# A recurrent attention and a routed expert layer on one core: experts in an order found on the chip, with a size for each place

## The chip, the cores and the metric

The program runs on one core of a Trainium2 chip, as one launch. The time is that of the launch in device microseconds; three runs of the kernel before took 530.75, 531.43 and 537.21 us, a median of 531.43 us. The core has TensorE (PE, matmuls; its weight loads have a row of their own, PEld), VectorE (DVE), ScalarE (ACT), GpSimd (POOL) and SyncE (SP, which only issues transfers here).

## What is computed

```python
# r, k, v: (4, 8, 768, 48); w, u: (8, 48); 8 experts, w1 (8, 384, 1024), w2 (8, 1024, 384), all float32
for t in range(S):                                    # attention, one state per batch and head
    y[:, :, t] = einsum('bhd,bhde->bhe', rt, state + (u * kt) outer vt)
    state = w * state + kt outer vt
x = y.transpose(0, 2, 1, 3).reshape(3072, 384)
logits = (x / |x|) @ (emb / |emb|).T / tau            # (3072, 8)
idx = argmax(logits);  gate = softmax(logits)[idx]
for e in range(8):
    h = maximum(x[idx == e] @ w1[e], 0)
    out[idx == e] = gate * (h @ w2[e])
```

Each of the 3072 tokens goes to exactly one expert.

## The kernel before

**Attention.** The sequence is cut into 6 groups of 128 positions (NCH, the index c), and each group into two turns of two batches (12 turns, index t). A turn scales and transposes R and K (scale_r, scale_k, turn_in, take_in, own_r), forms scores, masks them (mask, own_terms), adds the outer products of K and V to the state (outer, half_state, next_state), multiplies with V and with the state (with_v in two phases, with_state), and turns the result back into rows (take_y, turn_y, take_x), which keep_x stores to the array xs in HBM. The order of all this is written out by hand: attention() gives every function a planned time in a table (plan.at), and the functions are issued in the order of these numbers; on each engine the instructions then run strictly in that order, each waiting for what it reads.

**Routing.** After each second turn the 512 tokens of a group are routed: logits and take_logits (lgT), turn_logits and keep_logits (lg), choose (largest logit; VectorE steps mx, l, er, back, oh, a running count in counts), ranks (two small matmuls that count the tokens of the same expert before each token), placed (rank), places (tile and slot), gate, places_b (the one-hot arrays QV and P), put (matmuls that scatter token numbers and gates into lists) and collect (adds them to lists). The routing of a group is spread over the next turns; that of the last group has nothing beside it, and ends in take, the table of token numbers for each expert and tile.

**Experts.** Every expert has room for 512 tokens, four tiles of 128 (TM = 4); a place that no token fills has a number beyond the array and is skipped by the transfers. For each expert GpSimd gathers four tiles of rows from xs (gather, tiles G), TensorE transposes them (turn_x, three banks of four transposes, each copied by VectorE to xTe), layer1 does 8 x 3 matmuls with 512 columns into hT (ReLU on ScalarE), layer2 does 4 x 8 matmuls with 384 columns into the banks pu, VectorE scales by the gate, and GpSimd scatters the rows to the output. The order on TensorE is layer1(e), turn_x(e+1), layer2(e). The weights have two buffers. Those of experts 0 and 1 load in 14 pieces during turns 4 to 8 of the attention, those of expert e+2 as soon as layer1(e) and layer2(e) have let go of the buffer.

**The end.** needs() counts the tokens of each expert with one matmul and compares them with 512 x g; again() turns that into a flag that every engine loads into a register (line 963), and a branch that is not taken where all tokens had room (line 964). The branch holds a slow path for the tokens that did not fit.

## Time and profile before

| | us |
|---|---|
| median of three runs | 531.43 |
| the profiled execution | 535.02 |
| its span in the profile | 533.2 |
| TensorE busy in the span | 483.6 (91%) |
| VectorE, ScalarE, GpSimd busy | 143.9, 106.2, 137.5 |
| chain that ended last, layer 1 (L733) and layer 2 (L744) | 31% and 31% of the span |

The profile is one execution. A row names a line of the kernel, an engine, an operation and the tiles it writes and reads; times are microseconds from the start of the span. The releaser of a wait is inferred, and a wait that nothing in the profile explains is called "issue". The chain of work that ended last is followed back from the end, at each step to what released it.

### The profile page before, as it was taken

The numbers are of one execution on the slowest core, as the hardware profiler recorded it, in microseconds if no ns is written. First come the engines' busy times: TensorE is split into PE (matmuls) and PEld (weight loads), VectorE is DVE, ScalarE is ACT, GpSimd is POOL, SyncE is SP. The second block draws the span as 40 slices with busy tenths as digits, with TensorE's granted clock in tenths as the row PEclk, the third lists the DMA queues.
The fourth block names the chain that finished last, engine by engine and source line by source line (L and its number), as shares of the span: only waits on it lengthen the run. The fifth ranks groups of instructions, "written<-read, shape, count | busy, mean of one in ns | idle before, by whom it ended". The sixth has DMA issues, their size and how long they took to land.

```text
span 533.2 us, 10611 instructions
## 1 busy us (share of the span) xinstructions
PE 483.6 (91%) x4523; PEld 299.4 (56%) x4523; DVE 143.9 (27%) x390; ACT 106.2 (20%) x247; POOL 137.5 (26%) x167
## 2 busy tenths in 40 slices
PE   7889879888963999999999999999999999999990
PEld 3778768777852445545545545544554554554550
DVE  5656666676842110002001101101000200110010
ACT  1335535363450120020020021011012002002100
POOL 4447545355304401400310130230140110020010
PEclk9679999898995899999999999999999999999995
DMA  9938797994111312403223043142150330000000
GB/s 178 194 70 190 151 263 169 259 218 129 43 62 44 85 52 97 162 14 135 100 97 133 29 161 119 45 165 75 73 180 1 134 121 26 15 30 0 9 35 8
DMA packets 95515, 54.29 MB, mean 102 GB/s; under 512 B 78781, under 2 KB 90110, under 8 KB 95458
## 3 DMA queue, kind: packets, MB, share of 16 engines
q1 hardware_dynamic: 88658, 43.67, 29.6%
q0 software_dynamic: 4096, 9.45, 4.9%
q8 instruction: 37, 0.61, 0.5%
q10 hardware_dynamic: 2704, 0.40, 0.4%
q14 instruction: 20, 0.16, 0.1%
HBM read 45.63 MB, written 11.01 MB: 106 GB/s over the span
## 4 chain that ended last, share of the span: by engine, by line
PE 79%; DVE 8%; issue 3%; POOL 1%; DMA 1%; ACT 1%; POOLq 0%; DVEq 0%; ACTq 0%
PE ps L733 31%; PE pu L744 31%; PE ps L302 3%; PE pu L363 2%; PE py L724 2%; PE py L414 2%; PE ps L328 2%; PE py L433 2%; PE pu L448 1%; PE pu L596 1%; PE py L474 1%; DVE P L588 1%; DVE xTe L725 1%; DVE AT L342 1%; DVE RT L315 1%
## 5 line engine op out<-in xcount | busy, mean ns | idle before, releaser
L733 PE MATMUL ps<-xTe,w 128*128 128x512 f32 x384 | 167.6, 596 | 0.0
L744 PE MATMUL pu<-w,hT 128*128 128x384 f32 x512 | 166.4, 486 | 0.0
L744 PEld LDWEIGHTS pu<-w,hT 128*128 128x128 f32 x512 | 96.7, 190 | 66.2 <-issue 0.5
L733 PEld LDWEIGHTS ps<-xTe,w 128*128 128x128 f32 x384 | 73.6, 192 | 90.8 <-issue 89.0
L750 POOL DMA_INDIRECT out_dram<-y,take x32 | 31.8, 993 | 281.3 <-DVE y L749 277.2
L736 ACT ACTIVATE hT<-ps 128x512 f32<-128x512 f32 x64 | 38.2, 597 | 300.5 <-PE ps L733 300.5
L749 DVE TENSOR_SCALAR y<-pu,lists 128x384 f32<-128x384 f32 x32 | 19.7, 617 | 165.5 <-PE pu L744 165.5
L725 DVE COPY xTe<-py 128x512 f32<-128x512 f32 x24 | 15.9, 688 | 153.0 <-PE py L724 152.7
L711 POOL DMA_INDIRECT G<-xs,take x32 | 32.6, 1020 | 15.9 <-issue 8.2
L286 POOL TENSOR_TENSOR Rw<-R,rpow 128x384 f32<-128x384 f32 x24 | 24.8, 1034 | 22.1 <-PE ps L328 8.7
L328 PE MATMUL ps<-RT,KT 48*64 48x128 f32 x768 | 27.8, 297 | 0.8 <-issue 0.7
L328 PEld LDWEIGHTS ps<-RT,KT 48*64 48x64 f32 x768 | 24.3, 148 | 3.3 <-issue 2.7
L282 POOL TENSOR_TENSOR Kw<-K,kpow 128x384 f32<-128x384 f32 x24 | 25.5, 1062 | 0.0
L724 PE MATMUL py<-ident,G 128*128 128x128 f32 x96 | 15.6, 298 | 8.0 <-DMA G<-xs,take 5.5
L302 PE MATMUL ps<-ident,Rw 128*128 128x128 f32 x96 | 17.4, 306 | 3.7 <-POOL Rw L286 2.1
L309 ACT COPY RT<-ps 128x512 f32<-128x512 f32 x24 | 14.1, 586 | 30.9 <-PE ps L302 30.9
L315 DVE TENSOR_TENSOR RT<-ps,uw 128x512 f32<-128x512 f32 x24 | 16.4, 687 | 13.5 <-ACT RT L309 13.4
L724 PEld LDWEIGHTS py<-ident,G 128*128 128x128 f32 x96 | 11.7, 149 | 14.6 <-DMA G<-xs,take 6.5
L414 PE MATMUL py<-AT,V 64*64 64x64 f32 x768 | 18.8, 238 | 1.0 <-ACT peek L402 0.6
L342 DVE TENSOR_TENSOR AT<-ps,smask 128x256 f32<-128x256 f32 x48 | 17.8, 410 | 4.9 <-PE ps L328 4.9
L363 PE MATMUL pu<-V,Kw 64*64 64x48 f32 x704 | 15.6, 235 | 3.9 <-DVE full L550 2.0
L390 POOL TENSOR_TENSOR T<-T,wC 128x384 f32<-128x384 f32 x10 | 8.3, 827 | 40.2 <-DVE T L384 37.5
(142 smaller groups left out, 337.9 us busy)
## 6 DMA issues: line engine op xcount, KB each, us to landing
w<-in_moe_w_dram SPq DMA_DIRECT2D x24, 512.0 KB, 5.1
w<-in_moe_w_dram SPq DMA_DIRECT2D x32, 384.0 KB, 4.2
K<-in_k_dram SPq DMA_DIRECT2D x24, 192.0 KB, 4.0
V<-in_v_dram SPq DMA_DIRECT2D x24, 192.0 KB, 3.8
xs<-X SPq DMA_DIRECT2D x24, 192.0 KB, 2.9
R<-in_r_dram SPq DMA_DIRECT2D x22, 192.0 KB, 3.9
G<-xs,take POOLq DMA_INDIRECT x32, 3.4
out_dram<-y,take POOLq DMA_INDIRECT x32, 2.6
```

Of the source, the lines that this page charges most:

```text
L282: k.nc.gpsimd.tensor_mul(of(k.Kw, t)[:, u, :, 0:D], of(k.K, t)[:, u], k.kpow)
L286: ins = k.nc.gpsimd.tensor_mul(of(k.Rw, t)[:, u, :, 0:D], of(k.R, t)[:, u], k.rpow)
L302: k.nc.tensor.transpose(bank[:, p * C : (p + 1) * C], pair(src[:, u], p), k.ident)
L328: ins = k.nc.tensor.matmul(k.D[2 * u + par][halves(s), p * C : (p + 1) * C], KT[rows, u, p, halves(s)], RT[rows, u, p, s].rearrange("q j i ...
L363: k.nc.tensor.matmul(k.U[s][par * DP : (par + 1) * DP, col : col + D], Kw[halves(s), u, h, :], V[halves(s), u, h, 0:D], start=True, stop=T ...
L414: k.nc.tensor.matmul(y_out(k, par, p, u, s), V[halves(s), u, 2 * p + par, :], AT[halves(s), u, par, p * HC : (p + 1) * HC], start=first an ...
L711: k.nc.gpsimd.indirect_dma_start(out=G[:, :], out_offset=None, in_=k.xs[:, :], in_offset=IndirectOffsetOnAxis(ap=k.take[:, e, t : t + 1], ...
L724: k.nc.tensor.transpose(ps[:, t * 128 : (t + 1) * 128], G[:, m * 128 : (m + 1) * 128], k.ident)
L733: k.nc.tensor.matmul(ps, w1[:, m, f * 128 : (f + 1) * 128], xT[:, m, :], start=(m == 0), stop=(m == NK - 1))
L736: k.nc.scalar.activation(hT[:, f, :], ps, ACT.Relu)
L744: k.nc.tensor.matmul(ps, hT[:, f, t * 128 : (t + 1) * 128], w2[:, f, :], start=(f == 0), stop=(f == NF - 1))
L750: k.nc.gpsimd.indirect_dma_start(out=k.out[:, :], out_offset=IndirectOffsetOnAxis(ap=k.take[:, e, t : t + 1], axis=0), in_=y[:, :], in_off ...
```

## The change

The eight experts are run in an order that the chip finds, and each place j of the order has a fixed size, CAPS[j], in place of 512. After group 3 of the six the two experts with the fewest tokens so far become places 0 and 1 (settle, early); after group 4 the others follow by falling count, so that the largest sizes, 432, 416 and 400, stand at places 2 to 4. The order is a one-hot array; from it VectorE works out the experts' numbers (which), SyncE loads them into registers, and the weights are fetched at an address that the register gives (weights). The embeddings, the tie order, the running counts and the lists are put into the order by products and sums on VectorE (sort_embeddings, sort_counts, sort_lists), so that the last group routes straight into places. Expert 0's weights are now issued at the end of turn 10, expert 1's after the transposes of expert 0's rows. Sizes that are not whole tiles do layer 2 with the weights stationary and the rows streaming; their result yT is transposed back after the next expert's layer 1 (turn_out). needs compares the counts with the sizes.

The plan of the last turns and of the routing of groups 4 and 5 is written anew: outer and half_state of turn 11 stand at 4.1 and 4.5 of their turn where they stood at 4.75 and 5.6, and the 14 functions that routed group 5 one after another become a table of 17.

```diff
@@
+CAPS = (384, 384, 432, 416, 400, 384, 384, 384)
+EARLY = 2
+TILES = [-(-n // 128) for n in CAPS]
...
@@ def choose(k, c):
+def choose(k, c, rev=None):
...
+def scale(k, c):
+    inv = k.rt.tile([128, B], F32, name="inv", tag="inv")
+    k.nc.vector.reciprocal(inv, k.ssq[c % 2])
+    k.nc.vector.tensor_mul(k.shifted, k.shifted, over_e(inv))
...
@@ def ranks(k, c):
+    if c in SETTLE:
+        mm(bank[:, B * E : (B + 1) * E], k.ones, k.counts[:, :, B], start=True, stop=True)
...
+SETTLE = (NCH - 3, NCH - 2)
+def count(k, c):
+    k.nc.vector.scalar_tensor_tensor(
+        k.key, bank_of(k, "ranks", c)[:, B * E : (B + 1) * E], float(E), k.index if c == SETTLE[0] else k.rev,
+        ALU.mult, ALU.add,
+    )
+def settle(k, c):
...
+    if not early:
+        nc.vector.tensor_scalar(low, k.few, float(EARLY), -float(2 * E * N), ALU.is_lt, ALU.mult)
+        nc.vector.tensor_add(k.key, k.key, low)
+    nc.vector.tensor_tensor(
+        wins, k.key[:, None, :].to_broadcast(square), k.key[:, :, None].to_broadcast(square),
+        ALU.is_lt if early else ALU.is_gt,
+    )
+    nc.vector.reduce_sum(at, wins, axis=AX.X)
...
+def settled(k):
...
+    for j in range(js.start, js.stop):
+        k.expert[j] = k.nc.values_load(
+            k.which[0:1, j : j + 1], engines=(mybir.EngineType.SP,), min_val=0, max_val=E - 1,
...
+def in_order(k, out, a, n):
+    k.nc.vector.tensor_mul(
+        t, a[:, :, None, :].to_broadcast(shape), k.order[:, None, :, :].to_broadcast(shape)
+    )
+    k.nc.vector.reduce_sum(out, t, axis=AX.X)
+def sort_embeddings(k):
+    in_order(k, k.ent_sorted[:, :, 0:E], k.ent[:, :, 0:E], 4)
+def sort_counts(k):
+    in_order(k, k.rev_sorted[:, None, :], k.rev[:, None, :], 1)
+    in_order(k, k.cum[:, None, :], k.counts[:, None, :, B], 1)
+def sort_lists(k):
+    old, k.lists = k.lists, k.lists_sorted
+    shape = [128, E, 2 * TM, E]
...
@@ def attention(k):
-    for e in range(2):
-        for i, piece in enumerate(pieces(k, e, k.weights[e])):
-            plan.at((4 + 2 * e) * P + 1.0 + i * 4.0, piece)
+    plan.at((TURNS - 2) * P + 8.1, weights, k, 0)
...
+            plan.at(at + 4.1, outer, k, t)
+            plan.at(at + 4.5, half_state, k, t)
...
+def weights(k, j):
+    w1, w2 = k.weights[j]
+    e = bass.ds(k.expert[j], 1)
...
+def rows_in(e, t):
+    return min(128, CAPS[e] - 128 * t)
...
@@ def layer1(k, e):
-                ps, w1[:, m, f * 128 : (f + 1) * 128], xT[:, m, :], start=(m == 0), stop=(m == NK - 1)
+                ps, w1[:, m, f * 128 : (f + 1) * 128], xT[:, m, 0:n], start=(m == 0), stop=(m == NK - 1)
...
@@ def layer2(k, e):
+    for m in range(NK):
+        ps = k.U[m % 2][:, 0:n]
         for f in range(NF):
             k.nc.tensor.matmul(
+                ps, w2[:, f, m * 128 : (m + 1) * 128], hT[:, f, 0:n], start=(f == 0), stop=(f == NF - 1)
             )
+        k.nc.vector.tensor_copy(k.yT[:, m, 0:n], ps)
+def turn_out(k, e):
+    if CAPS[e] % 128 == 0:
+        return
+    for t in range(TILES[e]):
+        ps, n = k.U[t % 2][:, 0:DM], rows_in(e, t)
+        for m in range(NK):
+            k.nc.tensor.transpose(
+                ps[0:n, m * 128 : (m + 1) * 128], k.yT[:, m, t * 128 : t * 128 + n], k.ident
+            )
+        finish(k, e, t, ps)
...
@@ def experts(k):
+    ins = turn_x(k, 0)
+    after(k, weights(k, 1), ins)
     for e in range(E):
+        layer1(k, e)
+        if e:
+            turn_out(k, e - 1)
         if e + 1 < E:
             turn_x(k, e + 1)
...
@@ def needs(k, first):
+    nc.vector.tensor_tensor(many, cp[0:1, :], k.caps[0:1, :], ALU.is_gt)
+    nc.vector.tensor_mul(need, need, many[:, :, None].to_broadcast([1, E, TG]))
+    nc.vector.tensor_mul(
+        by, need.rearrange("o j g -> o g j")[:, None].to_broadcast(shape),
...
+    nc.vector.reduce_sum(need, by, axis=AX.X)
```

Three places, as the instructions stand in each engine's queue. The first is VectorE in the routing of the last group, from the running counts to the first step of places. Before:

```order
L521 SCALAR_TENSOR_TENSOR counts<-on,cum_oh 128x40
L523 RECIPROCAL inv<-ssq_139 128x4
L524 TENSOR_TENSOR l<-l,inv 128x32
L550 TENSOR_TENSOR full<-pu_62,cum_oh 128x32
L551 TENSOR_REDUCE rank<-full 128x4
L560 TENSOR_TENSOR over<-rank,level 128x16
```

and now (lists_sorted is the list in the new order):

```order
L546 SCALAR_TENSOR_TENSOR counts<-on,cum_oh 128x40
L655 TENSOR_TENSOR lists_by<-lists,order 128x512
L659 TENSOR_REDUCE lists_sorted<-lists_by 128x64
L665 TENSOR_TENSOR full<-ps_59,cum_oh 128x32
L666 TENSOR_REDUCE rank<-full 128x4
L675 TENSOR_TENSOR over<-rank,level 128x16
```

The reordering of the lists has moved in front of full, which reads the ranks, and the scaling inv and l has moved behind. The second is VectorE in the routing of group 4, from rank on. Before:

```order
L524 TENSOR_TENSOR l<-l,inv 128x32
L550 TENSOR_TENSOR full<-pu_62,cum_oh 128x32
L551 TENSOR_REDUCE rank<-full 128x4
L560 TENSOR_TENSOR over<-rank,level 128x16
L564 TENSOR_REDUCE hi<-over 128x4
L566 SCALAR_TENSOR_TENSOR lo<-hi,rank 128x4
L567 TENSOR_TENSOR over<-slot,hi 128x16
```

and now:

```order
L666 TENSOR_REDUCE rank<-full 128x4
L598 TENSOR_SCALAR low<-at 128x8
L599 TENSOR_TENSOR key<-key,low 128x8
L601 TENSOR_TENSOR wins<-key 128x64
L606 TENSOR_REDUCE at<-wins 128x8
L609 TENSOR_TENSOR order<-at,slot 128x48
L636 TENSOR_TENSOR by_turn<-ent,order 128x256
L639 TENSOR_REDUCE ent_sorted<-by_turn 128x4x8
L636 TENSOR_TENSOR by_turn<-rev,order 128x64
L639 TENSOR_REDUCE rev_sorted<-by_turn 128x8
L636 TENSOR_TENSOR by_turn<-counts,order 128x64
L639 TENSOR_REDUCE cum_oh<-by_turn 128x8
```

Between rank and the rest (over and what follows it) stand eleven operations that find the order and apply it, and after these rows come two more for the numbers in which. The third is TensorE at the end of the attention, where the logits of group 5 (L474, now L491) are formed and turned. L596 and L714 are puts, L448 and L465 the turn of YT_126 back into rows. Before:

```order
L596 MATMUL pu_63<-QV,P 128x64 x4
L448 MATMUL pu_62<-ident,YT_126 128x128 x4
L448 MATMUL pu_63<-ident,YT_126 128x128 x4
L474 MATMUL py_64<-YT_125,ent 32x128 x2
L474 MATMUL py_64<-YT_126,ent 32x128 x2
```

and now:

```order
L491 MATMUL py_64<-YT_126,ent_sorted 32x128 x2
L714 MATMUL ps_60<-QV,P 128x64 x4
L465 MATMUL pu_62<-ident,YT_126 128x128 x4
L465 MATMUL pu_63<-ident,YT_126 128x128 x4
L510 MATMUL ps_58<-ident,lgT 128x128
L574 MATMUL ps_59<-cum_oh,umask 128x32
```

The put of group 4 and the last turn of YT_126 have moved from ahead of the logits to behind them, ahead of the transpose of lgT.

## Rows read from the trace of the kernel before

**Rows 1.** Table by stage: start:end, length, engines' busy us (instructions), granted clock, DMA.

```profile
core 0: us, PE busy (x) PEld busy (x) DVE busy (x) ACT busy (x) POOL busy (x), PEclk, DMA share, GB/s
...
148.00:166.00 18.00, 10.66 (x227) 9.02 (x223) 9.68 (x46) 6.84 (x22) 1.27 (x2) 0.85 0.13 46
...
219.20:262.50 43.30, 42.95 (x126) 22.69 (x125) 4.45 (x7) 4.78 (x8) 8.06 (x8) 1.00 0.28 101
...
100.00:120.00 20.00, 18.18 (x548) 16.04 (x544) 12.31 (x39) 10.93 (x30) 7.33 (x9) 0.94 0.94 236
```

**Rows 2.** Chain that ended last, 174 to 243 us: start, duration, engine, tile, line.

```profile
174.76 22.09 PE ps L733 x48
...
198.73 20.64 PE pu L744 x64
219.37 20.60 PE ps L733 x48
239.97 0.45 PE py L724 x4
...
240.45 0.70 DVE xTe L725
...
241.19 0.66 PE py L724 x4
```

**Rows 3.** Timeline of VectorE, 141 to 150 us: start, duration, operation, [idle before, releaser].

```profile
141.85 0.29 DVE L482 COPY lgT<-py 128x128 f32<-128x128 f32 x1 [0.48 <-PE py L474]
...
143.25 0.68 DVE L588 TENSOR_TENSOR P<-slot,lo 128x512 f32<-128x512 f32 x1
...
148.76 0.56 DVE L379 TENSOR_TENSOR Tmid<-T,pu 128x384 f32<-128x384 f32 x1 [1.95 <-PE pu L363]
```

**Rows 4.** Timeline of VectorE, routing of the last group.

```profile
157.61 0.29 DVE L482 COPY lgT<-py 128x128 f32<-128x128 f32 x1 [1.86 <-PE py L474]
158.38 0.19 DVE L491 COPY lg<-pu 128x32 f32<-128x32 f32 x1 [0.48 <-PE pu L486]
...
159.75 0.24 DVE L521 TENSOR_TENSOR_SCAN counts<-on,cum_oh 128x40 f32<-128x40 f32 x1
...
162.39 0.43 DVE L582 TENSOR_TENSOR QV<-HV,cum_oh 128x256 f32<-128x256 f32 x1
162.74 0.68 DVE L588 TENSOR_TENSOR P<-slot,lo 128x512 f32<-128x512 f32 x1
165.54 0.19 DVE L604 TENSOR_TENSOR take<-lists,pu 128x32 int32<-128x32 f32 x1 [2.12 <-PE pu L596]
```

**Rows 5.** Timeline of TensorE, end of the attention.

```profile
154.39 1.10 PE L596 MATMUL pu<-QV,P 128*128 128x64 f32 x8 [0.54 <-DVE P L588]
155.33 1.13 PE L448 MATMUL pu<-ident,YT 128*128 128x128 f32 x8
...
163.56 1.94 PE L596 MATMUL pu<-QV,P 128*128 128x64 f32 x8 [3.10 <-DVE P L588]
```

**Rows 6.** Timeline of GpSimd, gathers for expert 0.

```profile
168.92 1.00 POOL L711 DMA_INDIRECT G<-xs,take  x1 [0.30 <-issue]
170.23 1.00 POOL L711 DMA_INDIRECT G<-xs,take  x1 [0.30 <-issue]
```

**Rows 7.** Timeline of TensorE in turn 5.

```profile
78.45 0.76 PE L302 MATMUL ps<-ident,Kw 128*128 128x128 f32 x3 [2.12 <-issue]
```

**Rows 8.** Table by stage, the stretch behind that gap; columns as in rows 1.

```profile
78.40:82.00 3.60, 3.55 (x100) 3.14 (x101) 0.02 (x1) 1.66 (x3) 0.00 (x0) 0.53 0.67 173
```

**Rows 9.** Line 701 (pieces of w1, 512 KB each), issue to landing.

```profile
DMA to landing us min/median/max: 3.4/5.1/7.7
```

**Rows 10.** Timeline of VectorE at the end.

```profile
519.90 0.52 DVE L786 TENSOR_SCALAR need<-ps 1x8 f32<-1x8 f32 x6
```

**Rows 11.** Line 963, register loads: ns min/median/max, first and last start.

```profile
L963 SPq TENSOR_LOAD <-flag x1: 465/465/465, 521.0 to 521.0; - x1
```

More of the change, by code (lines that the diff above doesn't have):

```diff
@@ L163, in build_consts @@
     k.slot = numbers(k, "slot", [128, 128], [[1, 128]], 0, 0)
+    k.index = numbers(k, "index", [128, E], [[1, E]], 0, 0)
+    k.caps = pool.tile([128, E], F32, name="caps")
+    nc.gpsimd.memset(k.caps, float(min(CAPS)))
+    for j, n in enumerate(CAPS):
+        if n > min(CAPS):
+            nc.gpsimd.memset(k.caps[:, j : j + 1], float(n))
+    k.order = pool.tile([128, E, E], F32, name="order")
+    k.which = pool.tile([1, E], I32, name="which")
+    k.ent_sorted = pool.tile([128, 4, 32], F32, name="ent_sorted")
+    nc.gpsimd.memset(k.ent_sorted, 0.0)
+    k.rev_sorted = pool.tile([128, E], F32, name="rev_sorted")
     k.level = numbers(k, "level", [128, TM], [[128, TM]], 128, 0)
@@ new lines, in settled @@
+def settled(k):
+    js = k.settled
+    n = js.stop - js.start
+    i = k.rt.tile([1, n, E], F32, name="index_of", tag=f"index_of{n}", bufs=1)
+    k.nc.vector.tensor_mul(i, k.order[0:1, js, :], k.index[0:1, None, :].to_broadcast([1, n, E]))
+    with k.nc.allow_low_precision(reason="small integers"):
+        k.nc.vector.reduce_sum(k.which[:, js], i, axis=AX.X)
+    for j in range(js.start, js.stop):
+        k.expert[j] = k.nc.values_load(
+            k.which[0:1, j : j + 1], engines=(mybir.EngineType.SP,), min_val=0, max_val=E - 1,
+            skip_runtime_bounds_check_because="an index of a one-hot row",
+        )
@@ L613, in attention @@
     P = PERIOD
+    end = (TURNS - 1) * P
     for t in range(TURNS):
@@ L669, in attention @@
-    end = NCH * 2 * P + 6.0
-    c = NCH - 1
-    for i, fn in enumerate((
-        logits, take_logits, turn_logits, keep_logits, choose_a, choose, exps, ranks, placed, places, gate,
-        places_b, put, collect,
-    )):
-        plan.at(end + (1.7 if i < 4 else 3.5) + 0.1 * i, fn, k, c)
+                plan.at(then + P + 3.95, collect, k, c)
+            if c == SETTLE[0]:
+                plan.at(then + 4.64, count, k, c)
+                plan.at(then + 7.4, settle, k, c)
+                plan.at(then + 7.45, settled, k)
@@ new lines, in attention @@
+    c = NCH - 2
+    for t, fn, *args in (
+        (1.0, choose_a, k, c),
+        (4.0, keep_logits, k, c),
+        (5.0, choose, k, c),
+        (6.3, scale, k, c),
+        (6.4, exps, k, c),
+        (6.5, ranks, k, c),
+        (6.7, count, k, c),
+        (6.75, placed, k, c),
+        (7.1, settle, k, c),
+        (8.2, sort_embeddings, k),
+        (8.9, sort_counts, k),
+        (9.3, settled, k),
+        (9.6, places, k, c),
+        (10.0, gate, k, c),
+        (10.1, values, k, c),
+        (10.2, rows_of, k, c),
+        (12.0 - 0.01, put, k, c),
+        (12.3, collect, k, c),
+    ):
+        plan.at(end + t, fn, *args)
@@ new lines, in attention @@
+    c = NCH - 1
+    for t, fn, *args in (
+        (11.0, logits, k, c),
+        (12.02, take_logits, k, c),
+        (12.92, turn_logits, k, c),
+        (12.93, keep_logits, k, c),
+        (13.0, choose, k, c, k.rev_sorted),
+        (14.3, ranks, k, c),
+        (14.35, sort_lists, k),
+        (15.4, placed, k, c),
+        (15.5, places, k, c),
+        (15.6, choose_a, k, c),
+        (15.7, scale, k, c),
+        (15.8, exps, k, c),
+        (15.9, rows_of, k, c),
+        (16.0, gate, k, c),
+        (16.1, values, k, c),
+        (16.2, put, k, c),
+        (16.3, collect, k, c),
+    ):
+        plan.at(end + t, fn, *args)
```

224 lines of the change are left out of this document (138 added, 86 removed).

## The prediction

> **What bounds the kernel now.** I read the table by stage first, then the chain of work that ended last, then the timelines of the places that the change rewrites. The table [rows 1] splits the program: from 219 us on TensorE is busy 42.95 of 43.30 us at a granted clock of 1.00 (the level of 2.4 GHz), so the expert stage is TensorE and nothing else; in the stretch ahead of it, 148 to 166 us, TensorE is busy 10.66 of 18 us, and VectorE, with 9.68 us in many small steps, is what the others wait for. The last 14 us of the program hold almost no work.
>
> The chain [rows 2] shows one expert: layer 1 takes 20.60 us (48 instructions), layer 2 20.64 us (64), and between them stand the turns of the next expert's rows, from 239.97 to layer 2 at about 241.85 us, 1.88 us. Each of the 48 streams 512 columns in 429 ns, each of the 64 streams 384 columns in 322.5 ns. Both are 0.8333 ns a column and 2.5 ns more, in the two passes that the row's count shows. So time follows columns, and the eight experts run 8 x 512 = 4096 padded rows for 3072 tokens. The stage before last is 8 x 41.24 + 7 x 1.88 + 1.5 = 344.6 us, from the first matmul to the last; the 1.5 us are the first layer at 22.09 us, while the clock was still coming up.
>
> **The change part by part.**
>
> *Columns.* The sizes add up to 3168. A size of 384 costs 48 x 322.5 ns = 15.48 us for layer 1 and the same for layer 2 (three tiles of 16). Sizes 432, 416, 400 cost 48 x 362.5, 349.2, 335.8 ns for layer 1, and layer 2, which for them has the weights stationary and the rows streaming, has 48 instructions of the same width. That is 5 x 30.96 + 34.80 + 33.52 + 32.24 = 255.4 us in place of 329.9: **74.5 us less**. Weight loads stay hidden under streams of 320 ns and more, as they are under these now.
>
> *Turns.* One turn is now four transposes, 0.45 us, a step to VectorE, a copy of 0.70 us, and the last four transposes [rows 2]. With three tiles the transposes take 0.34 us and the copy about 0.56: 1.52 us; with a narrow fourth tile 1.62 to 1.68. Seven turns: 11.0 us in place of 13.2, **2.2 us less**.
>
> *turn_out, new, three times.* Twelve transposes of 0.113 us with two banks, each bank waiting for its scaling (0.6 us) before it is used again, and the copies of the following turn_x queue behind four scalings on VectorE. Worked through: the fourth transpose group ends 2.1 us after layer 1, the fourth scaling at 2.95, the first xTe copy at 3.5, layer 2 starts at 3.95 us instead of 1.6. So 2.35 us each, **7.1 us more**. Bounds: 1.36 us each if all waits hide, 3.5 if none overlap.
>
> *Routing of the last two groups.* This is VectorE's queue. First, the early choice puts five small operations, and one more before them, ahead of the lgT at 141.85 us. Small dependent steps cost 0.23 us (six from 158.38 to 159.75, [rows 4]); lgT has 0.48 us to spare [rows 3]; so P of group 3, now at 143.25, is some 0.8 us later. Most of this is given back because the outer products go ahead of the second with_v: Tmid (148.76) shifts only 0.15 us. Second, after the counts of group 4 the queue holds, beside what stood there, key, low, key, wins, at, order, two operations for the embeddings (256 elements, 0.43 us like QV), four for the tie order and the counts, two for the index: by 0.23 us a step P of group 4 ends at about 157.8 us, where it ended at 154.3, and lgT can start only then (157.61 before, when it waited 1.86 us for TensorE). Third, the TensorE order now has group 4's put and the last turn_y, 1.10 and 1.13 us [rows 5], behind the logits and ahead of the turn of lgT; both stood ahead of the logits before. So lg comes at about 160.15 us, not 158.38: 1.8 us late. Fourth, two operations of 512 elements (0.68 us like P) and the scaling by the norm (inv, l) now stand in the chain from lg to take, less the 0.5 us in which VectorE waited for the ranks: 1.2 us. Sum **3.0 us more**. Bounds: 0 if the queue packs as it does now, 6 if each of the 20-odd added steps costs 0.3 us and none of them hides.
>
> *Gathers.* Three in place of four ahead of expert 0: the fourth issue is at 170.23, 1.31 us after the third [rows 6], but its rows land soon after; with shorter cold transposes (the put of group 5 took 1.94 us where group 4's took 1.10, [rows 5]) I take **0.9 us less** (0.4 to 2).
>
> *Weights by register.* The 6.3 MB that were loaded during the attention leave it. There the DMA engines stood at 0.94 of their time [rows 1], and TensorE had gaps that the trace names only "issue", the longest 2.12 us at 76.3 us [rows 7], after which it ran 3.6 us at a granted clock of 0.53 [rows 8], near the level of 1.2 GHz. If crowded DMA engines feed TensorE's instructions late, that gap is worth up to 2.1 + 1.7 = 3.8 us; but shorter gaps of the kind come before any weight is loaded. I take **1.0 us less**, between 0 and 3.8. The Trainium skill ("Runtime: NRT & Kernel Launch", Instruction fetch mechanics) says that the sequencer streams its instructions ahead by its own DMA queue and that crossing a block is mostly hidden; by that rule this term is 0 and the sum 1 us higher, and the 2.12 us gap is at odds with it.
>
> Expert 0's weights are issued about 143 to 147 us: two register loads of about 0.47 us [rows 11] behind the early choice. 3.1 MB at the 236 GB/s that the queue reached between 100 and 120 us [rows 1] is 13 us, so they land near 160; even at 101 GB/s, what the expert stage moves now, they land at 176, as layer 1 starts. Taken as 0. Six more register loads (2.8 us) hold the last three stores of X on SyncE until about 158.5 us and later; the last row block is only ready at 160.5, and the gathers start near 169, so 0 too. Expert 1's weights wait for expert 0's turns (176 us) and are wanted 32 us later. Afterwards 3.1 MB have some 33 us an expert, 95 GB/s; three pieces of 512 KB in flight landed in at most 7.7 us [rows 9], 204 GB/s. Taken as 0.
>
> *The end.* needs gains four operations on one partition, two of them of 384 elements: 0.15 + 0.2 + 0.55 + 0.55 us, less a memset; all engines wait for the flag behind them [rows 10, 11]. **1.35 us more** (1 to 2).
>
> *Sum*, against the span of 533.2 us: -74.5 - 2.2 + 7.1 + 3.0 - 0.9 - 1.0 + 1.35 = -67.15, a span of 466.0 us. The profiled execution took 535.02 us; the median of the runs is 531.43, 3.6 us below it, so the median after is **464.3 us**.
>
> **The rivals.**
>
> *An overflow.* If one expert has more tokens than its place's size, the program takes the slow branch. Counting the reference's router on its own inputs gives 352, 374, 427, 408, 386, 372, 373, 380 in the order found, against 384, 384, 432, 416, 400, 384, 384, 384: it decides from four tokens more. Price: 24 scatters of 1.3 us, eight experts' weights one after the other at 15.4 us, one expert of 41 us and its gathers: about 205 us, so 670 us and slower. Against it: the counts; rounding would have to move four tokens. 3 in 100.
>
> *Weights become the bound.* Below 95 GB/s an expert waits for its weights; below 73 GB/s it would be no faster than now. Against it stand 204 and 236 GB/s. At 90 GB/s the six late experts lose 2 us each: 477 us. 4 in 100.
>
> *The clock falls in the new gaps.* TensorE ran at 0.53 after the 2.12 us gap [rows 8], and at 1.00 through the present turns with 0.56 us of waiting. The turn_out places have about 1.6 us of waiting in pieces; if each costs 1.7 us of half clock, 5 us: 469 us. The Trainium skill ("TensorE: Matmul & The Clock Gate", Part 1) has the throttled state as the default, which activity lifts; that speaks for this rival, and the stretch at 0.53 agrees. 12 in 100.
>
> *The rewritten routing brings what it costs or more.* Were the shifts of the queue smaller and the attention's gaps gone, the stretch would end 3 to 4 us earlier than I have it: 460 us. 9 in 100.
>
> **How the numbers follow.** My forecast has 72 in 100. Its own bounds add up to about 7 us below and 9 above, and the clock and routing rivals lie within: **457 to 473 us**, which leaves out the weights, the overflow and a tenth of the forecast's own spread. Within 2% (about what can be told from no change) would be 521 to 542 us, where no case lies but a very slow weight load: 1 in 100. Faster 96, slower 3.
>
> **What would show it.** Right: layer 1 and layer 2 pieces of 15.5 us for five experts and 17.4, 16.8, 16.1 for three; about 4 us between layer 1 and layer 2 in three experts and 1.5 in the others; first expert matmul at 174 to 178 us; no wait of TensorE for w. Wrong: rows of a wait for w, a granted clock below 1.00 in the expert stage, an expert stage that does not end near 450 us, or a branch taken at the end.

## The result, and the profile after

The changed kernel takes **466.01 us** (median of 4 runs, 464.43 to 466.96) where the kernel before took 531.09 us in the same set (4 runs): a ratio of 0.875, 95% interval 0.868 to 0.883 (ratios are formed from means, so they differ a little from the quotient of the medians). The forecast was 464.3 us. In a later set of runs it took 465.54 us (463.36 to 467.31, 6 runs; ratio 0.873, 0.869 to 0.877). The profiled execution of 466.96 us has a span of 465.1 us; the span forecast was 466.0.

The chain of work that ended last, from the first expert on (start, duration, engine, tile, line). Line 908 is layer 1, 932 layer 2 with whole tiles, 940 layer 2 with the weights stationary, 952 the transposes of turn_out, 896 those of turn_x:

```profile
193.04 15.48 PE pu L932 x48
...
241.64 17.40 PE ps L908 x48
...
260.95 17.60 PE pu L940 x48
278.55 16.76 PE ps L908 x48
295.31 0.34 PE pu L952 x3
...
295.67 0.63 DVE y L918
...
298.06 0.49 DVE xTe L899
...
298.60 0.71 PE py L896 x4
299.31 16.96 PE pu L940 x48
316.26 16.12 PE ps L908 x48
...
402.59 0.34 PE py L896 x3
...
404.12 15.48 PE pu L932 x48
```

It answers to [rows 2]. A piece with 384 columns takes 15.48 us, and 17.40, 16.76 and 16.12 us stand for 432, 416 and 400 columns. Between layer 1 of 416 columns, which ends at 295.31, and the next layer 2 at 299.31 lie 4.00 us, since y must be scaled (line 918) before its bank takes the next transposes, and xTe queues behind it. The two other such places take 3.83 and 3.82 us; a turn of three whole tiles takes 1.53 (402.59 to 404.12).

The table by stage, answering to [rows 1]: the weights' first transfers during the routing, and the expert stage.

```profile
core 0: us, PE busy (x) PEld busy (x) DVE busy (x) ACT busy (x) POOL busy (x), PEclk, DMA share, GB/s
138.80:147.80 9.00, 6.62 (x244) 5.95 (x247) 6.66 (x29) 1.62 (x6) 0.00 (x0) 0.89 0.98 338
175.20:450.60 275.40, 272.33 (x879) 157.73 (x878) 32.72 (x58) 32.09 (x64) 46.96 (x48) 1.00 0.33 111
```

In the expert stage TensorE is busy 272.33 of 275.40 us at a granted clock of 1.00; no row of it waits for w. In the 9 us from 138.8 the DMA engines stand at 0.98, 338 GB/s. That is expert 0's weights, beside the routing of group 4.

TensorE at the end of the attention, which answers to [rows 5]:

```profile
135.81 1.98 PE L345 MATMUL ps<-RT,KT 48*64 48x128 f32 x64
...
144.49 0.39 PE L572 MATMUL ps<-counts,ones 128*128 128x8 f32 x2 [1.48 <-DVE counts L546]
...
147.40 0.56 PE L450 MATMUL py<-RT,T 48*48 48x64 f32 x10 [0.82 <-issue]
...
152.59 1.98 PE L491 MATMUL py<-YT,ent_sorted 128*32 128x128 f32 x32 [0.70 <-ACT YT L457]
154.50 1.97 PE L714 MATMUL ps<-QV,P 128*128 128x64 f32 x8
156.26 1.91 PE L465 MATMUL pu<-ident,YT 128*128 128x128 f32 x8
...
164.93 1.97 PE L714 MATMUL ps<-QV,P 128*128 128x64 f32 x8 [4.06 <-DVE QV L705]
...
175.15 2.18 PE L908 MATMUL ps<-xTe,w 128*128 128x384 f32 x4
```

In the kernel before the scores of turn 11, the logits of the last group and the first matmul of expert 0 stand here:

```profile
141.71 1.98 PE L328 MATMUL ps<-RT,KT 48*64 48x128 f32 x64
...
156.39 1.08 PE L474 MATMUL py<-YT,ent 128*32 128x128 f32 x32
...
174.55 10.71 PE L733 MATMUL ps<-xTe,w 128*128 128x512 f32 x21
```

The granted clock of after falls between these two stages (columns as in the table by stage):

```profile
143.00:146.00 3.00, 1.52 (x52) 1.46 (x54) 2.08 (x13) 1.40 (x4) 0.00 (x0) 0.98 1.00 374
146.00:149.00 3.00, 2.18 (x65) 1.82 (x58) 2.61 (x12) 0.07 (x1) 0.00 (x0) 0.50 0.94 337
```

And VectorE, which answers to [rows 4]:

```profile
158.43 0.19 DVE L515 COPY lg<-ps 128x32 f32<-128x32 f32 x1 [1.70 <-PE ps L510]
...
166.94 0.19 DVE L722 TENSOR_TENSOR take<-lists_sorted,ps 128x32 int32<-128x32 f32 x1 [2.06 <-PE ps L714]
```

The scores of turn 11 (line 345) start at 135.81 us; in the kernel before, the same row (line 328) is at 141.71. So up to there the attention is 5.90 us shorter in this pair of traces. But from there to take pass 31.13 us, where 23.83 passed before. TensorE waits 1.48 us for counts, until 144.49; from 146.0 us on the granted clock is 0.50; from 146.58 to 147.40 (0.82 us) TensorE waits for nothing that the profile shows. At that clock every product takes nearly twice its time: the logits 1.98 us instead of 1.08, put 1.97 instead of 1.10, the turn of YT 1.91 instead of 1.13. From take to the first matmul of expert 0 (175.15 us) pass 8.21 us, 9.01 before. The first expert thus starts 0.60 us later than before: -5.90 + 7.30 - 0.80.

VectorE at the end, answering to [rows 10]:

```profile
450.60 0.62 DVE L918 TENSOR_SCALAR y<-pu,lists_sorted 128x384 f32<-128x384 f32 x1 [4.54 <-PE pu L932]
...
451.97 0.84 DVE L998 TENSOR_TENSOR need_by<-need,order 1x384 f32<-1x384 f32 x1
452.84 0.54 DVE L1003 TENSOR_REDUCE need<-need_by 1x48 f32<-1x384 f32 x1
...
453.82 0.14 DVE L1177 CAST flag<-some 1x1 int32<-1x1 f32 x1
```

From the last y to flag pass 3.22 us; before it was 1.51 (519.37 to 520.88).

### The profile page after: what moved, and what is told of

It is laid out like the page before. It is cut to its first block, busy times and chain, and to the rows that moved or that the text cites. A ratio compares the mean times of both kernels' runs of the same rounds, so it can differ in the third digit from the quotient of the medians.

```text
span 465.1 us, 10536 instructions
## 1 busy us (share of the span) xinstructions
PE 412.8 (89%) x4420; PEld 277.0 (60%) x4420; DVE 149.4 (32%) x420; ACT 100.7 (22%) x247; POOL 128.1 (28%) x163
## 4 chain that ended last, share of the span: by engine, by line
PE 76%; DVE 10%; issue 3%; POOL 1%; ACT 1%; DMA 1%; POOLq 0%; DVEq 0%
PE ps L908 28%; PE pu L932 17%; PE pu L940 11%; PE ps L319 3%; PE pu L380 3%; PE ps L345 2%; PE pu L465 2%; PE py L896 2%; PE py L450 2%; PE py L431 2%; PE py L491 1%; DVE P L691 1%; DVE RT L332 1%; DVE y L918 1%; DVE AT L359 1%
## 5 line engine op out<-in xcount | busy, mean ns | idle before, releaser
L908 PE MATMUL ps<-xTe,w 128*128 128x384 f32 (+3 forms) x384 | 129.7, 498 | 0.0
L919 POOL DMA_INDIRECT out_dram<-y,take x27 | 26.7, 988 | 222.9 <-DVE y L918 183.5
L911 ACT ACTIVATE hT<-ps 128x384 f32<-128x384 f32 (+3 forms) x64 | 32.1, 501 | 240.2 <-PE ps L908 212.0
L932 PE MATMUL pu<-w,hT 128*128 128x384 f32 x240 | 78.3, 486 | 0.0
L932 PEld LDWEIGHTS pu<-w,hT 128*128 128x128 f32 x240 | 45.3, 190 | 30.8
L918 DVE TENSOR_SCALAR y<-pu,lists_sorted 128x384 f32<-128x384 f32 (+3 forms) x27 | 16.1, 615 | 131.9 <-PE pu L932 84.0
L940 PE MATMUL pu<-hT,w 128*128 128x432 f32 (+2 forms) x144 | 51.0, 514 | 0.0
L940 PEld LDWEIGHTS pu<-hT,w 128*128 128x128 f32 x144 | 27.1, 190 | 22.0 <-issue 15.3
L899 DVE COPY xTe<-py 128x384 f32<-128x384 f32 (+3 forms) x24 | 13.3, 565 | 72.2 <-PE py L896 72.0
L943 DVE COPY yT<-pu 128x432 f32<-128x432 f32 (+2 forms) x9 | 5.3, 592 | 45.4 <-PE pu L940 45.4
```

The lines of the kernel that those rows point to most:

```text
L908: k.nc.tensor.matmul(ps, w1[:, m, f * 128 : (f + 1) * 128], xT[:, m, 0:n], start=(m == 0), stop=(m == NK - 1))
L911: k.nc.scalar.activation(hT[:, f, 0:n], ps, ACT.Relu)
L919: k.nc.gpsimd.indirect_dma_start(out=k.out[:, :], out_offset=IndirectOffsetOnAxis(ap=k.take[0:n, e, t : t + 1], axis=0), in_=y[0:n, :], in ...
L932: k.nc.tensor.matmul(ps, hT[:, f, t * 128 : (t + 1) * 128], w2[:, f, :], start=(f == 0), stop=(f == NF - 1))
L940: k.nc.tensor.matmul(ps, w2[:, f, m * 128 : (m + 1) * 128], hT[:, f, 0:n], start=(f == 0), stop=(f == NF - 1))
```

## The experiments

Below, "the stretch" is the time from the scores of turn 11 to take in the profiled execution. The kernel before gave medians of 534.23, 534.18 and 532.78 us in the three sets of runs, so each ratio is to the one of its set.

| kernel | median us (range, runs) | ratio to before, 95% | scores, turn 11 | take | stretch | first expert |
|---|---|---|---|---|---|---|
| before | 531.43 | | 141.71 | 165.54 | 23.83 | 174.55 |
| after | 466.01 (464.43-466.96, 4) | .875 (.868-.883) | 135.81 | 166.94 | 31.13 | 175.15 |
| after again | 465.54 (463.36-467.31, 6) | .873 (.869-.877) | 137.51 | 166.20 | 28.69 | 174.36 |
| all 512 | 534.90 (531.70-537.42, 10) | 1.001 (.998-1.004) | 133.53 | 164.65 | 31.12 | 173.65 |
| full tiles | 480.66 (479.48-483.38, 4) | .903 (.898-.909) | 133.96 | 164.75 | 30.79 | 172.91 |
| fixed addresses | 465.63 (462.50-467.58, 4) | .871 (.865-.877) | 133.12 | 165.37 | 32.25 | 173.51 |
| early weights | 467.94 (466.23-470.58, 4) | .878 (.872-.883) | 138.97 | 165.88 | 26.91 | 174.01 |
| before, late weights | 529.00 (525.02-534.21, 10) | .990 (.987-.994) | 135.99 | 160.73 | 24.74 | 169.72 |
| filler | 466.49 (465.40-467.21, 5) | .873 (.869-.878) | 134.36 | 163.21 | 28.85 | 173.76 |
| order | 465.41 (462.24-467.20, 6) | .872 (.867-.876) | 133.80 | 161.28 | 27.48 | 169.56 |
| later | 466.92 (464.55-468.83, 6) | .875 (.871-.879) | 133.04 | 159.45 | 26.41 | 171.70 |
| all three | 466.44 (465.35-469.10, 6) | .874 (.870-.878) | 133.92 | 163.15 | 29.23 | 174.48 |
| fitted filler | 461.96 (458.81-465.67, 6) | .869 (.863-.874) | 133.04 | 160.29 | 27.25 | 168.37 |
| order and fitted filler | 460.59 (458.52-462.51, 6) | .865 (.861-.869) | 133.96 | 159.55 | 25.59 | 167.56 |

The stage marks are from one execution each. In the two profiles of after and the nine variants of it that load the weights late, the scores start between 133.04 and 137.51 us, so a single difference of 1 or 2 us in that column says nothing.

**Which part of the change gives the time: all sizes 512.**

```diff
-CAPS = (384, 384, 432, 416, 400, 384, 384, 384)
+CAPS = (512, 512, 512, 512, 512, 512, 512, 512)
```

> The changed kernel with all eight sizes at 512: no narrow tile, no turn_out, columns and gathers as before; the order, the weights by register and the rewritten routing stay. Theory (time follows columns): the expert stage is 344 to 345 us again from the first to the last matmul, and the time is 466 + 69.6 + 0.9 = 536.5 us, 534 to 539. So without the sizes the change is slower than before (531.1 us) by some 3 to 7 us. Rival (the late weights gain more than the routing costs): 528 to 531 us.

1.001 of the kernel before (0.998 to 1.004). The found order, the late weights, the register loads, the new plan and the longer needs together cost or gain nothing that shows; the sizes are the whole gain that shows. The expectation of 3 to 7 us more than before did not come true; 534.90 lies in its range of 534 to 539 only because before took 534.23 in this set, not the 531.1 that it was added to.

**The ragged sizes: three full tiles more.**

```diff
-CAPS = (384, 384, 432, 416, 400, 384, 384, 384)
+CAPS = (384, 384, 512, 512, 512, 384, 384, 384)
```

> The changed kernel with 512 columns instead of 432, 416 and 400 in the three largest experts; so they need no turning at the end. The prediction's terms: two pieces an expert cost 20.6 instead of 17.4, 16.8 and 16.1 us, together +23.0; the turning of gathered tiles with a few columns more +0.9; three turnings of output at 2.35 each fall away, -7.1. Sum +16.8: 482.8. If the turning cost less in the sum than the gap of 4 us shows (work beside it), 485 or more; if the clock had suffered from it, 480 or less.

480.66 us, 15.1 above after in the same set. Its chain, a turn between two large experts:

```profile
239.60 20.60 PE ps L908 x48
...
262.08 20.64 PE pu L932 x64
```

Layer 1 and layer 2 take 20.60 and 20.64 us, the turn between them 1.88 (239.60 + 20.60 to 262.08). In the trace of after the six pieces of the three ragged experts take 101.0 us, here 123.7: 22.8 us for the columns, which agrees with 23.0. The three places of turn_out take 4.00, 3.83 and 3.82 us there, and the same three places take 1.88, 1.53 and 1.53 here (303.32 to 305.20, 346.44 to 347.97, 384.09 to 385.62): 6.7 us, not 7.1. The 0.9 us for wider tiles in the turns is not there: turns with a full fourth tile take 1.87 and 1.88 us here, those with a narrow one 1.95 and 1.91 there. The whole stage is 291.6 us, first matmul to last, against 275.4: +16.2, expected 16.8.

**The registers: fixed addresses.** The numbers that the chip finds for these inputs are written into the code; nothing is loaded into registers for the weights.

```diff
-    for j in range(js.start, js.stop):
-        k.expert[j] = k.nc.values_load(
...
-    e = bass.ds(k.expert[j], 1)
+    e = (0, 5, 4, 3, 1, 7, 2, 6)[j]
```

> The changed kernel with the weights fetched at the same places from fixed addresses in the same order (0, 5, 4, 3, 1, 7, 2, 6), without the eight register loads on SyncE; VectorE still works out the order. Theory: register loads and computed addresses are hidden, 465 to 467 us, and expert 0's first piece is issued some 1 to 2 us earlier. Rival: the register loads hold back the stores of X or the weights and cost something at the end of the attention: 463 us or less.

465.63 us, as after within the spread. The loads by register cost nothing that can be measured, which was the forecast.

**When the weights load: the change with early weights, the kernel before with late ones.** In the first, places 0 and 1 get the weights of the experts that stand there (0 and 5) in pieces during turns 4 to 7, as before. In the second, the kernel before issues them where after does.

```diff
-    plan.at((TURNS - 2) * P + 8.1, weights, k, 0)
+    for e in range(2):
+        for i, piece in enumerate(pieces(k, (0, 5)[e], k.weights[e])):
+            plan.at((4 + 2 * e) * P + 1.0 + i * 4.0, piece)
```

> The changed kernel, with one part undone: the weights of the first two experts load in pieces during turns 4 to 8 of the attention as before, from the addresses of experts 0 and 5, which are those that the order finds on these inputs. In the changed kernel the scores of turn 11 begin at 135.81 us, 5.90 us earlier than before (141.71), and from there to take it needs 31.13 us, 7.30 more than before (23.83). Theory A, the weights crowd the DMA engines during the attention and TensorE's gaps named issue grow with them: the scores of turn 11 move back to 141 to 142 us. Rival B, the attention got shorter by the new plan of its last turns: they stay near 136. For the stretch from the scores to take: if the weights that now load there cause its 0.82 us gap in TensorE and the low clock behind it, it shrinks to 27 to 28 us and the time is 468 to 470 us; if the long VectorE queue alone does it, it stays at 31 and the time is 471 to 473 us. Under B the time is 466 us or less.

467.94 us. With the weights in the attention the scores of turn 11 are at 138.97, 1.5 to 6 us later than in any variant with late weights, but between the 141 to 142 of theory A and the 136 of rival B; so this run alone doesn't settle how much of the 5.90 us is the weights. Its ratio (0.872 to 0.883) isn't separated from that of after: what the late weights gain in the attention is mostly lost in the routing. The stretch takes 26.91 us. VectorE there:

```profile
157.37 0.19 DVE L515 COPY lg<-ps 128x32 f32<-128x32 f32 x1 [0.77 <-PE ps L510]
...
165.88 0.19 DVE L722 TENSOR_TENSOR take<-lists_sorted,ps 128x32 int32<-128x32 f32 x1 [2.06 <-PE ps L714]
```

lg comes 18.40 us after the scores and take 8.51 us after lg. The forecast had 18.44 and 8.36: the stretch is 3.1 us longer than the 23.83 of before, forecast 3.0, once no weights load beside it. Not all of that is the queue: here too the granted clock is 0.50 from 149 to 152 us. With the weights issued later (below) it is 1.00 until lg is there; lg then comes 17.91 us after the scores and the stretch is 26.41, 2.6 us more than before.

```diff
-    for e in range(2):
-        for i, piece in enumerate(pieces(k, e, k.weights[e])):
-            plan.at((4 + 2 * e) * P + 1.0 + i * 4.0, piece)
+    for piece in pieces(k, 0, k.weights[0]):
+        plan.at((TURNS - 2) * P + 8.1, piece)
```

> The kernel before, with one part of the change alone: the weights of expert 0 are issued at the end of turn 10 and those of expert 1 behind the transposes of expert 0's rows, from fixed addresses; order, sizes and routing are those of before. Theory A (crowded DMA engines): the scores of turn 11 begin at 135.5 to 136.5 us instead of 141.71, and the time falls from 531.1 to about 525 us if the stretch from there to take keeps its 23.8 us; if weights in that stretch lengthen it too, by a gap and half clock as in the changed kernel, the time is 527 to 529 us. Rival B (the new plan of the last turns): scores at 141 to 142 us and 530 to 532 us.

529.00 us, 0.990 of before (0.987 to 0.994): late weights are worth 5.2 us by the medians, 5.72 at the scores of turn 11, in a kernel in which nothing else is changed. Of the 5.72 us between the two traces, 4.2 are less busy time of TensorE from 30 us to the scores (99.34 and 95.09 us, at a mean clock of 0.94 and 0.98), the rest is less idle time. The stretch grows by 0.91 us alone, although the DMA engines are nearly as crowded there (0.94 from 136 to 148 us). TensorE and its clock (columns as in the tables by stage):

```profile
135.99 1.98 PE L328 MATMUL ps<-RT,KT 48*64 48x128 f32 x64
...
147.55 0.44 PE L433 MATMUL py<-RT,T 48*48 48x64 f32 x17 [0.64 <-issue]
...
149.39 1.10 PE L596 MATMUL pu<-QV,P 128*128 128x64 f32 x8
```

```profile
136.00:148.00 12.00, 9.58 (x328) 8.42 (x327) 8.36 (x36) 4.21 (x16) 1.36 (x2) 1.00 0.94 325
...
146.00:149.00 3.00, 2.03 (x111) 1.74 (x113) 2.55 (x12) 1.29 (x8) 0.00 (x0) 1.00 0.57 205
```

There is a gap of 0.64 us too, but the clock is 1.00 through it: put takes 1.10 and the logits 1.08 us. So the 7.30 us of after are two things: 2.6 to 3.1 for the new order of the queues, and some 4 that go with the half clock. The second part varies: in after again the clock is back at 1.00 from about 153.6 us, put of group 4 takes 1.10 us, and the stretch is 28.69, 1.8 us more than with early weights.

**Is it the clock? Filler.** Products of a constant tile that nobody reads are put into TensorE's gaps; warm(k, n) issues n of them.

```diff
+        (6.45, warm, k, 10),
         (6.5, ranks, k, c),
...
+        (10.95, warm, k, 8),
         (11.0, logits, k, c),
...
+        (14.25, warm, k, 10),
         (14.3, ranks, k, c),
...
+        (16.15, warm, k, 30),
         (16.2, put, k, c),
...
+            if e == 0 and m == 0:
+                warm(k, (28, 5, 4)[t])
```

> The changed kernel with filler on TensorE alone: products of a constant tile that nobody reads, in the gaps of the last group's routing (10 ahead of ranks of group 4, 8 ahead of its last logits, 10 and 30 ahead of ranks and put of group 5, 28, 5 and 4 ahead of the first three pieces of turning the first gathered tiles). Theory 'half clock': the 4 us that the weights add to the stretch from the scores of turn 11 to take are lost because the granted clock is 0.50 there, so logits, put, turn_y and the last put take 1.9 to 2.0 us each instead of 1.1. With the clock kept at 1.00 put(4), turn_y and logits take 1.1, lgT comes 2.5 us sooner, and with the last put and the turning of the first expert the median is 461 to 462. Rival 'VectorE's queue': the stretch waits for VectorE's new order whatever the clock; then the clock is 1.00 and the median still 465 or more. Rival 'issue gap': what matters is the wait of 0.8 to 1.1 us of TensorE near 146; then 1 us or less is won.

466.49 us: no gain, and yet the clock is 1.00 from 131 to 179 us (0.974 over the span, 0.939 in after). TensorE:

```profile
155.39 6.94 PE L966 MATMUL ps<-ones 128*128 128x128 f32 x60
162.17 1.00 PE L714 MATMUL ps<-QV,P 128*128 128x64 f32 x8
163.01 6.47 PE L966 MATMUL ps<-ones 128*128 128x128 f32 x56
169.31 0.27 PE L902 MATMUL py<-ident,G 128*128 128x128 f32 x1
```

and VectorE:

```profile
152.99 0.19 DVE L515 COPY lg<-ps 128x32 f32<-128x32 f32 x1 [0.77 <-PE ps L510]
...
159.02 0.42 DVE L705 TENSOR_TENSOR QV<-HV,cum_oh 128x256 f32<-128x256 f32 x1
```

lg comes 18.63 us after the scores instead of 22.62: the 4 us are back. Then the filler itself spends them. QV ends at 159.44, but the filler ahead of put runs until 162.2; the filler ahead of the first turned tile runs until 169.3, where 163.21 (take) + 3.91 as in after would be 167.1. By the figures on record this is the outcome of the rival 'VectorE's queue' (clock 1.00, median 465 or more); the trace speaks against it, since lg did come 4 us sooner. If so, the miss was in the numbers of the filler, which the fitted filler below tests.

**The order.** The turn of lgT goes ahead of the last turn_y and of put of group 4, collect behind ranks of group 5.

```diff
-        (12.0 - 0.01, put, k, c),
-        (12.3, collect, k, c),
+        (12.5, put, k, c),
+        (14.32, collect, k, c),
...
-        (12.02, take_logits, k, c),
-        (12.92, turn_logits, k, c),
-        (12.93, keep_logits, k, c),
+        (11.1, take_logits, k, c),
+        (11.2, turn_logits, k, c),
+        (11.3, keep_logits, k, c),
```

> The changed kernel with another order of the last group's routing: the turn of lgT ahead of the last turn_y and of put of group 4 on TensorE, and collect of group 4 behind ranks of group 5. Theory 'half clock': put (1.97 us) and turn_y (1.91 us) at half clock no longer stand between the logits and lgT, so lgT comes some 3.5 us sooner; part of it is taken back by collect behind it; take comes 1.5 to 3 us sooner and the median is 463 to 464.5. Rival 'VectorE's queue': VectorE's operations from lgT to take are a chain of their own of some 12 us, and its start moves by the whole 3.5 us: 462.5. Rival 'nothing': the order of put and lgT is hidden behind VectorE's lists of group 4: 465 to 467.

465.41 us by the median: the difference to after is inside the spread, so by itself the order is not shown to gain, as the rival 'nothing' had it. The profiled execution was the fastest of the six and has a stretch of 27.48. The six stand in one order by time and by the clock over the span: 462.24 us at 0.958, 463.04 at 0.950, 464.32 at 0.947, and 466.50, 466.68 and 467.20 at 0.940. That speaks for the clock as the source of the spread.

**Later weights.**

```diff
-    plan.at((TURNS - 2) * P + 8.1, weights, k, 0)
+    plan.at(end + 9.35, weights, k, 0)
```

> The changed kernel with the first expert's weights issued later: behind the register loads, ahead of the last three stores of X on SyncE's queue, so that they load some 8 us later. Theory 'weights beside the routing': the weights' transfers at a DMA share of 0.9 to 1.0 make the gap of some 1 us near 146 after which the clock is 0.50; without it the stretch from the scores of turn 11 to take is 27 us, as it was with the early weights (26.9), and take comes near 162.5: 461 to 462.5. Rival 'weights late for the first expert': the two tiles land 8 us later, still ahead of the first matmul at 174 if their transfers take under 20 us; if they take longer, TensorE waits for them there and the median is 466 to 470. Rival 'moved only': gap and half clock come 8 us later, at the last logits and put, and the median is 464 to 466.

466.92 us. The stretch is 26.41, as the first theory had it (27), there is no gap, and the clock is 1.00 from 138 to 153 us. But the gathers do not follow take (159.45). GpSimd and the chain:

```profile
163.87 1.28 POOL L883 DMA_INDIRECT G<-xs,take  x1 [9.12 <-issue]
```

```profile
154.89 7.88 DMA xs<-X
```

The first gather starts at 163.87, after a wait of 9.12 us, because the last store of X, issued behind the weights on SyncE's queue, lands 7.88 us after its issue at 154.89; in after no store of X took more than 4.9. None of the three theories on record had that: I had looked for the price at the weights and not at what stands behind them in the queue.

**All three together**, with the first filler:

> Filler, order and later weights together in the changed kernel. Theory 'half clock': the filler and the later weights take away the same 4 us, the order another 1.5 to 2: 459 to 461. Rival 'VectorE's queue': the order alone counts, 462.5 to 464.5. Rival 'nothing adds': no better than the best of the three alone.

466.44 us. It has both prices: take at 163.15 (the filler ahead of put), and the first gather at 164.49, 1.34 us after take where it was 0.49 with the filler alone. The rival 'nothing adds' was right.

**The filler fitted to the gaps**, alone and with the order, beside the changed kernel once more. The diff is against the first filler; with the order, 2 and 19 stand in place of the second 6 and of the first 16:

```diff
-        (6.45, warm, k, 10),
+        (6.45, warm, k, 6),
...
-        (10.95, warm, k, 8),
+        (10.95, warm, k, 3),
...
-        (14.25, warm, k, 10),
+        (14.25, warm, k, 6),
...
-        (16.15, warm, k, 30),
+        (16.15, warm, k, 16),
...
-                warm(k, (28, 5, 4)[t])
+                warm(k, (16, 4, 3)[t])
```

> The changed kernel as it is, once more, beside the three kernels below: 466, the spread between executions 464 to 467 (a theory of the last group's routing has to explain that spread too: 'half clock' says the shorter executions are those whose granted clock over the span is higher).

> The changed kernel with filler as before, but fitted to the gaps (6, 3, 6, 16 products ahead of ranks, logits, ranks and put, 16, 4 and 3 between the first pieces turned), since the first filler kept the clock at 1.00 and brought lg 4.0 us sooner, but held put back by 2.7 us and the turning of the first tiles by some 2.5. Theory 'half clock': with 1.00 to the first expert, lg is 4 us sooner, put 1.0 instead of 2.0, the turning some 1 us and the first expert's first pieces some 1 us shorter: 460 to 461. Rival 'what the gaps hide comes back elsewhere' (VectorE's queue, the landing of the gathered tiles): 464 or more.

> The order (the turn of lgT ahead of the last turn_y and of put of group 4) and the fitted filler (6, 3, 2, 19; 16, 4, 3) together. Theory 'half clock' and order together: order alone gave 465.4 with take 3.7 us sooner after the scores than in the changed kernel in the one trace; at full clock lg comes another 1.5 to 2 us sooner than by the filler alone: 458.5 to 460. Rival 'nothing adds': as the filler alone, 460 to 461. Rival 'bound elsewhere': 464 or more.

461.96 us alone and 460.59 with the order, 3.6 and 5.0 below the 465.54 of after in the same set. Both miss their expected ranges (460 to 461, 458.5 to 460) by 1.0 and 0.6 us. The intervals of the second and of after (0.861 to 0.869, 0.869 to 0.877) just meet, and its slowest execution (462.51) is below the fastest of after (463.36). It is the fastest kernel of the study. TensorE and VectorE of the second:

```profile
145.00 0.55 PE L450 MATMUL py<-RT,T 48*48 48x64 f32 x23 [0.76 <-issue]
...
153.81 4.49 PE L966 MATMUL ps<-ones 128*128 128x128 f32 x38
158.41 1.10 PE L714 MATMUL ps<-QV,P 128*128 128x64 f32 x8
...
167.56 10.88 PE L914 MATMUL ps<-xTe,w 128*128 128x384 f32 x33
```

```profile
151.43 0.19 DVE L515 COPY lg<-ps 128x32 f32<-128x32 f32 x1 [0.42 <-PE ps L510]
...
159.55 0.19 DVE L722 TENSOR_TENSOR take<-lists_sorted,ps 128x32 int32<-128x32 f32 x1 [1.20 <-PE ps L714]
```

put of group 5 takes 1.10 us instead of 1.97 and ends where the filler lets it; take is 25.59 us after the scores, and the first expert starts at 167.56, 8.01 after take, at full clock. The gap of 0.76 us is still there. So what the filler takes away is the half clock and not the gap. Fitted filler alone left more to chance: three executions took 458.8 to 459.4 us and three 464.6 to 465.7. Its median lies between the two, and its interval (0.863 to 0.874) overlaps that of after, so by itself it is not shown to gain; the gain is shown for filler and order together.

The executions of after (clock over the span 0.937 to 0.954) vary by 4 us. The fastest, 463.36, is the one with 0.954, but 463.67 had 0.943 and 464.99 had 0.946; the clock explains a part of the spread at most.

## Why the prediction was right, and where it was wrong

**The expert stage** came out step by step. Pieces of 15.48, 17.40, 16.76 and 16.12 us stand in the rows as worked out from 0.8333 ns a column and 2.5 ns; layer 2 of the ragged experts takes 0.2 us more in two of the three. The places of turn_out take 3.8 to 4.0 us, forecast 3.95; net of the plain turns in the run with full tiles they cost 6.7, forecast 7.1. A turn with a narrow fourth tile takes 1.91 to 1.95 us, not the 1.62 to 1.68 that I took. From the first matmul to the last it is 275.4 us, forecast 275.0.

**The start of the expert stage** was forecast at 175.65 us (174.55 + 3.0 - 0.9 - 1.0) and is at 175.15. That is luck, right for a wrong reason: two terms were wrong and cancelled.

- *Weights out of the attention*, taken as -1.0 with a bound of -3.8, is -5.9 in the trace of after and -5.2 by the medians of the kernel before with late weights. The step that failed is the bound: it counted the one gap of 2.12 us [rows 7] and the half clock behind it [rows 8]. With late weights more than that one place is shorter: the mean clock from 30 us to the scores is 0.98 where it was 0.94. The sentence on the Trainium skill ("Runtime: NRT & Kernel Launch", Instruction fetch mechanics) gave 0 for this term; 5.2 us are there. That late instructions are the cause isn't shown, since no run took the fetch alone away, so what the skill says of the fetch isn't refuted either.
- *Expert 0's weights beside the routing* were "taken as 0", since they land in time. They do; but they cost about 4 us in another way. Late weights in the old plan cost 0.91 us in the stretch, in the new plan 31.13 - 26.91 = 4.2 in one pair of traces, and 1.8 to 5.3 over the five traces of this routing (after twice, all 512, full tiles, fixed addresses). What takes the time is the granted clock of 0.50, half of full speed (1.2 GHz), during logits, put and turn_y, which in this plan stand on the path to lg.

**Routing**, forecast +3.0, is +3.1 where no weights load beside it. The step from scores to lg (18.44 forecast, 18.40 found) and from lg to take (8.36, 8.51) both hold, though some 0.5 us of it is the half clock of that run. In after itself lg alone is 4.2 us later.

**Gathers** -0.9: -0.80 from take to the first matmul. **Registers** 0: as forecast; the eight loads took 0.26 to 0.53 us each, with a median of 0.27, not 0.47. **The end** +1.35: flag comes 1.71 us later behind the last y (need_by takes 0.84 us where 0.55 was taken). Behind flag the span ends 11.3 us later instead of 12.3. It is 11.2 to 11.4 in the other kernels with sizes below 512 but two (11.8 with the first filler, 12.1 with all three), and 12.3 again with all 512; I had no term for that 1 us and no run explains it. So the end costs 0.7 net.

**From the span to the median.** The span came out at 465.1 us, forecast 466.0, but the median at 466.01, forecast 464.3. The step between them took 3.6 us off, because the profiled execution of before lay that far above a median of three runs; that of after lies 0.95 above its own. With the medians of before in the later sets (532.78 to 534.23) the same -67.15 gives 465.6 to 467.1. The bounds of the terms add up to 10 us below the forecast (3.0, 3.0, 1.1, 2.8, 0.35), not 7; nothing hung on it.

**The rival "the clock falls in the new gaps"** had the right mechanism at the wrong place. At the three turn_out places the clock stays at 1.00. It falls at the routing, behind TensorE's wait of 1.48 us for counts. The Trainium skill ("TensorE: Matmul & The Clock Gate", Part 1) has half clock as the default that activity lifts; the filler agrees, 1.00 from 131 to 179 us and 0.974 over the span; in after, on the other hand, the clock stayed at 0.50 while TensorE was busy without a pause from 152.6 to 158.4 us. **Weights as the bound**: no row waits for w. **Overflow**: no branch is taken.

What stays open is what exactly lets the clock fall. The new plan leaves TensorE a wait of 1.46 to 1.48 us for counts, which the old one does not have (in the kernel before with late weights no wait in that place is over 0.74). Where this wait was followed by a gap of 0.2 to 1.1 us (after twice, all 512, full tiles, fixed addresses, order), the clock fell to 0.50 in every trace. But in three of the six it fell ahead of that gap, which then can't have set it off: in after (0.50 from 146.0 us, the gap from 146.58), in after again (from 147 at the latest, the gap from 148.86) and with fixed addresses (from 142.5 at the latest, the gap from 145.64; there another gap, of 0.65 us, stands ahead of the wait). The rows of after stand above; those of after again and of fixed addresses are:

```profile
147.00:148.50 1.50, 1.50 (x51) 1.44 (x54) 1.16 (x7) 0.00 (x0) 0.00 (x0) 0.50 1.03 343
```

```profile
142.50:144.00 1.50, 1.50 (x10) 1.44 (x14) 0.20 (x2) 0.33 (x2) 0.00 (x0) 0.50 0.51 176
```

With the wait alone it fell with early weights and did not with later ones. With filler in the wait and a gap of 0.76 it did not fall, with one of 1.04 it fell for some 3 us; with neither (first filler, all three) it did not. So it fell once with the wait alone, in three traces ahead of the gap, and once with the gap alone; the wait that the new plan makes is the likelier start in after, but neither settles it. No run takes the gap alone away by design, and what makes the gap isn't shown.

## What to carry to other kernels

Where TensorE bounds a stage at full clock, price a change of padding by columns and the hand-overs by their chain of bank and queue; both could here be had from the rows of before to within 1 us. A load that lands in time is not free on that account: ask what it runs beside, and whether TensorE there has waits that let the clock fall. Filler that nobody reads can hold the clock, but only as much of it as the gap has room for; each product too many is paid in full, as the first filler showed.

## What I had not expected of the hardware

- Two tiles of weights, 3.1 MB, moved at 338 GB/s with the DMA engines at 0.98 of their time, well above the 236 GB/s that I had taken [rows 1]: some 9 us.
- A product over one partition with a broadcast of 384 elements (need_by) took 0.84 us on VectorE, its sum 0.54; the 512-element product on 128 partitions P takes 0.69.
- With the clock at 0.50 the small products of the routing take nearly twice their time (put 1.97 against 1.10 us, logits 1.98 against 1.08), and the clock stayed there though TensorE was busy without a pause from 152.6 to 158.4 us.
